# Tile 2's hidden layer from seven half-size products, its preparation moved into the searched list

## The chip, the cores and the metric

The kernel runs on one core of a Trainium2 chip. The metric is the time on the device in microseconds (us), median of several runs; the kernel before takes 837.97 us (three runs, 837.77 to 838.3). A profile is one more execution, taken by the hardware profiler.

## The reference

Attention in chunks of 64 tokens, then a two-layer network with h·cos(h) between the layers. In the core of it:

```python
scores = scale * np.matmul(q_c, k_c.transpose(0, 1, 2, 4, 3))   # chunks of 64 tokens, 8 heads of 64
attn = np.exp(scores - np.max(scores, axis=-1, keepdims=True))
attn = attn / (np.sum(attn, axis=-1, keepdims=True) + 1e-09)
x = np.matmul(attn, v_c)          # laid out as (4608 tokens, 512)
h = x @ w_in                      # (4608, 512) @ (512, 2048)
g = h * np.cos(h)
out = g @ w_out                   # (4608, 2048) @ (2048, 512)
```

All of it is float32.

## The kernel before, in words

The 4608 tokens are nine tiles of 512 (tile 0 to tile 8). The 2048 hidden features are 16 blocks of 128 (`fc`). To keep float32 accuracy at the fast matmul format, every operand is kept as a high and a low part, and every product is three matmuls: high·high, high·low, low·high.

**Ordinary tiles.** For one block, `hidden` (line 514) issues 12 matmuls of 512 columns into one PSUM bank of the pair named `h`; `activated` (525) makes g = h·cos(h) in six steps that alternate between ScalarE (ACT) and VectorE (DVE): whole turns, minus those turns, sine, times h (after which the bank is free), high part, low part. `projected_by_parts` (564) multiplies g with the block of w_out: four parts of three 512-column matmuls into the four banks `acc`. The projection of a step follows its hidden product three steps later (`LAG`).

**Pairs of blocks by seven products.** From tile `FAST` on, two blocks are taken together (`pair`, 776): h of the two is a two-by-two block product that is formed from seven products of half size (A11, S3, S2, A12, A22, S1, S4 in that order, six matmuls of 256 columns each) and a few additions. It needs seven combinations of x (`halves`, 707: four differences on DVE, seven high parts on ACT, seven low parts on DVE) and seven of w_in for each of eight pairs of blocks. The combinations of w_in are formed once, on GpSimd (POOL) with the high parts on ACT (`whole_again`, `sums_of_w`, `parts_of_sums`, 645 to 670), kept in HBM (`combo`), and streamed back for every tile, two products (512 KB) a load, through `load_two` (696) into rooms that the resident w_in leaves free. Room `fc` is free once the four sums of its pair have gone out (`keep_sums`, 681). SyncE (SP) issues every DMA in program order.

**What sets the order.** The kernel begins with a list of pieces (`piece`, 1001): weight preparation, attention of tiles 0 to 2, and hidden and projection of tile 0 (blocks 0 to 7), tile 1, and tile 0 again (blocks 8 to 15), which is 32 hidden steps and 29 projections. `in_order` (138) places the pieces by assumed lengths and due times, then tries 1,500 random changes of the due times and keeps what ends no later. After the list, tile 2 runs in a written loop (1249 to 1274) as an ordinary tile: beside its 16 steps the loop issues the attention of tile 3 (two bursts of small matmuls, `burst`, 964), the combinations of x for tile 3 and of w_in for the pairs 0 to 4. Tiles 3 to 8 run through `pair`; the pairs 5 to 7 of w_in are combined during the first of them. Before the first pair of a tile, `run_of_short` (913) issues the scores of the next tile, a run of 128 small matmuls into both `h` banks and both `a` banks; DVE's `m` (largest, 384) and `e` (scores minus largest, 388) read them out and free the banks, and the first product A11 needs one of the two `h` banks.

Of the kernel before, what the change touches and what calls it, by code (L numbers as in the profile page):

```python
# [21 lines left out]
P = 128  # L22
# [8 lines left out]

GROUP = 8


SCORES = 0
WEIGHTED = 12
LAST_TURN = 5

FAST = 3


STREAM = 5
# [1 line left out]

H_ROOM = 3
G_ROOM = 4
X_ROOMS = {1: (0, 1, 2), 0: (13, 14, 15)}

EARLY = 2

# [15 lines left out]
IDLE = 3.0  # L66

AHEAD = 4.0
TRIALS = 1500


def placed(work, after_it, rank):
# [65 lines left out]
def in_order(work, next_tile):  # L138

    after_it = [[] for _ in work]  # L140
    for i, w in enumerate(work):
        for a in w[3]:
            after_it[a].append(i)
    matmuls = [i for i, w in enumerate(work) if w[0] == PE and w[1] > LONG]

    due = [1e9] * len(work)
    clock = 0.0
    for i in matmuls:
        due[i] = clock
# [12 lines left out]
    chance = random.Random(1)  # L162
# [11 lines left out]
def attention_then_cos_ffn(ctx: ExitStack, tc, qT, kT, v, w_in, w_out, out, wide):  # L174
# [25 lines left out]
    def kept(ins):  # L200
        tc.keep_in_program_order(ins)
        return ins
# [337 lines left out]
            lambda: kept(nc.vector.tensor_tensor(g_lo, g, g_hi.bitcast(F32), op=ALU.subtract)),  # L540
        ]

    def activate(t, fc, h, most):
        whole, turn, sine, times, high, rest = activated(t, fc, h)
        whole()
        turn()
        take(soon, 1)
        sine()
        times()
        take(soon, 1)  # L550
        take(full, 2)
        high()
        rest()
        take(full, len(full))
        take(soon, most)
        take(late, len(late))

    def project(s):
        sums_out = []
        for run in projected_by_parts(s, sums_out):  # L560
# [28 lines left out]
    def finish(t, sub, o, whole):  # L589
        r0 = t * TOK + sub * P  # L590
        to = out[r0 : r0 + P, :]
        if not whole:

            os, to = att.tile([P, DM], F32, name="vt" if sub % 2 else "pts"), partial[sub]
        elif t == 0:
            os = acc["partial", sub]
        elif t < NT - 1 and t != FAST - 1:
            os = out_room(sub)
        else:

            if sub % 2 == 0:
                acc["x"] = x_room(t + 2 if t < FAST else t + 1, F32)
            os = acc["x"][:, sub % 2]
        if whole and t == 0:
            kept(nc.vector.tensor_tensor(os, os, o, op=ALU.add))
        elif t < FAST - 1 and sub % 2 == 0 or t == NT - 1 and sub % 2:
            kept(nc.scalar.copy(out=os, in_=o))
        else:
            kept(nc.vector.tensor_copy(os, o))
        nc.sync.dma_start(out=to, in_=os)  # L610

    def resume():

        for sub in range(NSUB):
            os = acc["partial", sub] = out_room(sub)
            nc.sync.dma_start(out=os, in_=partial[sub])

# [19 lines left out]

    sums_w = {}  # L640

    def pool(out, a, b, op):
        kept(nc.gpsimd.tensor_tensor(out, a, b, op=op))

    def whole_again(k):

        one, two = in_halves(k)
        for j, a in ((A11, one[:, :, 0]), (A12, one[:, :, 1]), (A22, two[:, :, 1])):
            store(combo(k, j), a)
        sums_w[k] = [dec.tile([P, 2, HALF], F32, name="w") for _ in range(2)]  # L650
        for w, a in zip(sums_w[k], (one, two)):
            pool(w, a[:, 0].bitcast(F32), a[:, 1].bitcast(F32), ALU.add)

    def sums_of_w(k):
        w1, w2 = sums_w[k]
        u, v = sums_w[k] = [wts.tile([P, 2, HALF], F32, name=f"half{i}") for i in range(2)]
        pool(u[:, 0], w2[:, 0], w2[:, 1], ALU.add)
        pool(u[:, 1], w1[:, 0], w2[:, 0], ALU.subtract)
        pool(v[:, 0], u[:, 0], w1[:, 0], ALU.subtract)
        pool(v[:, 1], w1[:, 1], v[:, 0], ALU.subtract)  # L660

    def parts_of_sums(k):

        one, two = in_halves(k)
        u, v = sums_w.pop(k)
        rooms = [(u[:, 0], two[:, :, 0]), (u[:, 1], one[:, :, 0]), (v[:, 0], one[:, :, 1]), (v[:, 1], two[:, :, 1])]
        for a, room in rooms:
            kept(nc.scalar.copy(out=room[:, 0], in_=a))
        for a, room in rooms:
            pool(room[:, 1], a, room[:, 0].bitcast(F32), ALU.subtract)  # L670

    def combine(k):

# [33 lines left out]
    def halves(t):  # L707
# [40 lines left out]
    def halves_in_turn(t):  # L748
        difference, high, low = halves(t)
        return [  # L750
            lambda: (difference(S1), high(A11)), lambda: (difference(S3), high(S1)),
            lambda: (difference(S2), high(S3)), lambda: (difference(A22), high(S2)),
            lambda: (low(A11), high(A12)), lambda: (low(S3), high(A22)), lambda: (low(S2), high(S4)),
            lambda: low(A12), lambda: low(A22), lambda: low(S1), lambda: low(S4),
        ]


    due_parts = deque()
# [202 lines left out]

    pieces = {}

    def attend(t, step):

        if step == 9:
            for hp in range(2, HP):
                load_v(t, hp)
        if step == 3:
            soon.extend(lambda hp=hp: total(t, hp) for hp in range(HP))  # L970
            soon.append(lambda: inverse(t))

        for hp in {4: (0, 1), 5: (2,), 6: (3,)}.get(step, ()):
            soon.append(lambda hp=hp: quotient(t, hp))
        if 4 <= step < 12:
            hp, odd = divmod(step - 4, 2)
            if not odd:
                pieces["turn"] = turned(t, hp)
            soon.extend(pieces["turn"][4 * odd : 4 * odd + 4])

    def burst(t, scored):


# [141 lines left out]
    ahead = early(1)  # L1125


    def attend_third(begin, room):

        t = 2  # L1130
        below = []
        for g in range(2):
# [16 lines left out]
        for g in range(2):  # L1149
# [14 lines left out]
            if g == 0:  # L1164
# [1 line left out]
                    for hp in (2, 3):  # L1166
                        load_v(t, hp)
                piece(SP, 0.1, values_next, w)
            for i in (0, 2):
                hi = piece(ACT, 0.45, rest_of(key, i), w, room)  # L1170
                banks_free["a", i // 2] = piece(DVE, 0.6, rest_of(key, i + 1), hi)
                x_done.setdefault(t, []).append(banks_free["a", i // 2])

        def queries_next():
            for hp in range(HP):
                load_qk(t + 1, hp)

        def values_after():
            for hp in range(2):
                load_v(t + 1, hp)  # L1180

        piece(SP, 0.1, values_after, piece(SP, 0.1, queries_next, w))


    stream = None
# [2 lines left out]
    projected = {}  # L1188
    partial_out = []
    out_of = {}  # L1190
    for s in range(STAGE):
        t, fc = order[s]
        key = ("h", s)
# [11 lines left out]
        if s >= LAG:  # L1205
# [9 lines left out]
            if order[u + 1][0] != tu:  # L1215
                for sub in range(NSUB):
                    done = piece((DVE if sub % 2 else ACT), 0.6, rest_of(key, sub), stream,
                                 *(split.values() if u > GROUP else [ahead[HP - 1]]))
                    out_of[u + 1, sub] = done
                    if u < GROUP:  # L1220
                        partial_out.append(done)
                if u < GROUP:
# [4 lines left out]
                else:  # L1227
                    piece(SP, 0.1, resume, *(out_of[u + 1, sub] for sub in range(NSUB)))
# [9 lines left out]
        given[s] = a  # L1238
        if s == GROUP + 7:
            begin = hid  # L1240
        if s == GROUP + NFC - 1:
            attend_third(begin, hid)

    for i in in_order(work, x_done[2]):
        work[i][2]()


    through = STAGE - 1 - LAG
    for s in range(STAGE, STAGE + NFC):
        t, fc = order[s]  # L1250
        h = hidden(t, fc)
        attend(t + 1, fc)
        if s - LAG > through:
            through += 1
            full.extend(project(through))
        if fc in (SCORES, WEIGHTED):
            burst(t + 1, fc == SCORES)
            through += 1
            full.extend(project(through))
        activate(t, fc, h, {WEIGHTED + 1: 2, WEIGHTED + 2: 0, WEIGHTED + 3: 1}.get(fc, 4))  # L1260
        if fc == WEIGHTED:
            soon.extend(halves_in_turn(t + 1))
            prefetch(t + 2)
            take(soon, 2)
        if fc == 2:
            exponentials(t + 1)
        take(full, len(full))

        if fc in (3, 5, 7, 9, 11):
            combine((fc - 3) // 2)  # L1270
        if fc == 13:
            parts_of_sums(4)
        if fc >= 7 and fc % 2:
            keep_sums((fc - 7) // 2)
# [82 lines left out]
```

## Time and profile before

| | |
|---|---|
| median of three runs | 837.97 us |
| profiled execution | 837.58 us |
| its span, first to last instruction | 835.8 us |
| mean granted TensorE clock | 0.998 |
| busy: PE / weight loads / DVE / ACT / POOL | 819.9 / 712.0 / 632.9 / 462.9 / 82.0 us |
| chain that ended last | PE 87%, ACT 5%, DVE 4%, DMA 2% |

The profiled execution lies 0.39 us under the median of the runs, and 1.78 us of it lie outside the span. Times in rows are us from the span's start. PE is the matmul engine, PEld its weight loads. In the chain of waits, "x12" counts matmuls that are merged into a row.

### The profile page before, as it was taken

The page shows a single profiled execution, that of the slowest core. Times are in us where ns is not written, and L with a number is a line of the kernel's source. Part 1 is how long each engine was busy: PE and PEld are TensorE (multiplying, and loading weights), DVE is VectorE, ACT ScalarE, POOL GpSimd, SP SyncE. Part 2 cuts the span into 40 slices and gives each one's busy share as a digit, 9 for nine tenths or more (in the row PEclk, how much of TensorE's full clock was granted, in tenths as well). Part 3 has the DMA queues.
Part 4 walks back from the last instruction along what each step waited for, and adds up shares of the span by engine and source line. Part 5 has one row for each costly group of instructions (what it writes and reads, how often), then busy time and mean ns, then how long its engine had stood idle before and what let it go on. Part 6 is the DMA issues. An engine that isn't in the chain of part 4 may idle for free.

```text
span 835.8 us, 16892 instructions
## 1 busy us (share of the span) xinstructions
PE 819.9 (98%) x6656; PEld 712.0 (85%) x6656; DVE 632.9 (76%) x1198; ACT 462.9 (55%) x928; POOL 82.0 (10%) x92
## 2 busy tenths in 40 slices
PE   5999999999999999999999999999999999999998
PEld 5777888888888878888998899889988899899996
DVE  6969888843698589977898788968896889665443
ACT  5999973333434636564645564465446454644443
POOL 1010000000069454400000000000000000000000
PEclk9999999999999999999999999999999999999999
DMA  9991200430245678986856675676657575456521
GB/s 338 415 414 43 77 1 1 134 118 1 79 161 202 213 228 313 325 316 209 277 175 227 202 257 177 206 240 210 215 179 249 189 250 177 152 176 227 177 76 50
DMA packets 65998, 160.47 MB, mean 192 GB/s; under 512 B 6528, under 2 KB 20864, under 8 KB 65920
## 3 DMA queue, kind: packets, MB, share of 16 engines
q1 hardware_dynamic: 65920, 159.41, 55.5%
q8 instruction: 52, 0.85, 0.4%
q14 instruction: 26, 0.21, 0.1%
HBM read 134.22 MB, written 25.17 MB: 191 GB/s over the span
## 4 chain that ended last, share of the span: by engine, by line
PE 87%; ACT 5%; DVE 4%; DMA 2%; issue 1%; SPq 0%; ACTq 0%; DVEq 0%
PE acc L208 44%; PE h L208 42%; DMA w_in<-in_w_in_dram 2%; PE a L208 1%; DMA qt<-in_qT_dram 1%; ACT half L278 1%; ACT w L276 1%; DVE g L536 1%; ACT g_hi L539 0%; ACT g L537 0%; DVE g L538 0%; SPq L205 0%; ACT g L535 0%; ACT w_out L286 0%; ACT L395 0%
## 5 line engine op out<-in xcount | busy, mean ns | idle before, releaser
L208 PE MATMUL acc<-w_out,g_hi 128*128 128x512 f32 x960 | 299.5, 393 | 0.0
L208 PE MATMUL h<-x,w_in 128*128 128x256 f32 (+1 forms) x1728 | 290.1, 317 | 2.0 <-DVE e L388 1.6
L208 PEld LDWEIGHTS h<-x,w_in 128*128 128x128 f32 x1728 | 255.3, 188 | 34.5 <-issue 2.3
L208 PEld LDWEIGHTS acc<-w_out,g_hi 128*128 128x128 f32 x960 | 171.8, 188 | 31.0
L208 PE MATMUL acc<-w_out,g_lo 128*128 128x512 f32 x480 | 187.4, 390 | 0.0
L827 ACT ACTIVATE g<-g 128x256 f32<-128x256 f32 x144 | 70.6, 490 | 113.8 <-DVE g L823 113.8
L208 PE MATMUL h<-w_in,w_in 128*128 128x256 f32 x864 | 118.5, 281 | 0.5 <-DVE w_in L814 0.4
L208 PEld LDWEIGHTS h<-w_in,w_in 128*128 128x128 f32 x864 | 110.8, 188 | 6.5 <-DVE w_in L814 3.0
L208 PEld LDWEIGHTS acc<-w_out,g_lo 128*128 128x128 f32 x480 | 90.1, 188 | 19.7
L811 ACT COPY h<-h 128x256 f32<-128x256 f32 x96 | 34.3, 357 | 117.4 <-PE h L208 115.9
L208 PE MATMUL acc<-w_out,w_in 128*128 128x512 f32 x288 | 73.7, 393 | 0.0
L842 DVE TENSOR_TENSOR g_lo<-g,g_hi 128x512 fp32r<-128x512 f32 x72 | 49.2, 686 | 22.7 <-ACT g_hi L838 21.6
L814 DVE TENSOR_TENSOR w_in<-h,w_in 128x256 f32<-128x256 f32 x96 | 36.2, 419 | 36.6 <-ACT x L740 18.7
L208 PEld LDWEIGHTS acc<-w_out,w_in 128*128 128x128 f32 x288 | 51.1, 188 | 8.8
L451 DVE STREAM_TRANSPOSE pts<-e 32x256 f32<-32x256 f32 x128 | 55.5, 435 | 1.9
L536 DVE SCALAR_TENSOR_TENSOR g<-g,h 128x512 f32<-128x512 int32 x48 | 32.8, 684 | 30.5 <-ACT g L535 29.9
L535 ACT ACTIVATE g<-h 128x512 int32<-128x512 f32 x48 | 28.6, 595 | 41.8 <-PE h L208 41.7
L830 DVE TENSOR_TENSOR g<-w_in,g 128x512 f32<-128x512 f32 x48 | 34.3, 714 | 17.4 <-ACT g L827 17.4
L539 ACT CAST g_hi<-g 128x512 fp32r<-128x512 f32 x48 | 29.9, 622 | 30.0 <-DVE g L538 25.1
L540 DVE TENSOR_TENSOR g_lo<-g,g_hi 128x512 fp32r<-128x512 f32 x48 | 35.5, 740 | 14.4 <-ACT g_hi L539 13.1
L830 DVE TENSOR_TENSOR g<-h,g 128x256 f32<-128x256 f32 x96 | 40.3, 420 | 8.0 <-ACT g L827 7.0
L823 DVE SCALAR_TENSOR_TENSOR g<-g,h 128x256 f32<-128x256 int32 x96 | 39.8, 415 | 8.6 <-ACT g L820 8.0
(108 smaller groups left out, 924.3 us busy)
## 6 DMA issues: line engine op xcount, KB each, us to landing
w_in<-combo SPq DMA_DIRECT2D x168, 512.0 KB, 3.9
combo<-w_in SPq DMA_DIRECT2D x56, 256.0 KB, 4.5
qt<-in_qT_dram SPq DMA_DIRECT2D x36, 256.0 KB, 5.1
kt<-in_kT_dram SPq DMA_DIRECT2D x36, 256.0 KB, 5.3
w_in<-in_w_in_dram SPq DMA_DIRECT2D x16, 512.0 KB, 9.6
w_out<-in_w_out_dram SPq DMA_DIRECT2D x16, 512.0 KB, 9.9
vt<-in_v_dram SPq DMA_DIRECT2D x22, 256.0 KB, 4.7
out_dram<-w SPq DMA_DIRECT2D x14, 256.0 KB, 2.1
```

The costliest lines, as they stand in the source:

```text
L208: kept(nc.tensor.matmul(*args, **kw))
L451: kept(nc.vector.transpose(out=dst[o : o + BL, :, qb], in_=src[i : i + BL, :, kb]))
L535: lambda: kept(nc.scalar.activation(n, h, AF.Identity, bias=0.25, scale=0.5 / math.pi)),
L536: lambda: kept(nc.vector.scalar_tensor_tensor(g, n, -2.0 * math.pi, h, op0=turns, op1=over)),
L539: lambda: kept(nc.scalar.copy(out=g_hi, in_=g)),
L540: lambda: kept(nc.vector.tensor_tensor(g_lo, g, g_hi.bitcast(F32), op=ALU.subtract)),
L811: kept(nc.scalar.copy(out=out, in_=in_))
L814: kept(nc.vector.tensor_tensor(out, in_, ds, op=ALU.add))
L823: kept(nc.vector.scalar_tensor_tensor(g, g.bitcast(I32), -2.0 * math.pi, h, op0=ALU.mult, op1=ALU.add))
L827: kept(nc.scalar.activation(g, g, AF.Sin, bias=0.5 * math.pi))
L830: kept(nc.vector.tensor_tensor(g, h, g, op=ALU.mult))
L842: kept(nc.vector.tensor_tensor(lo, g, hi.bitcast(F32), op=ALU.subtract))
```

## The change

`FAST` becomes 2, so tile 2 goes through `pair` as well and its written loop is gone. What the loop did is in the list now: the combinations of x for tile 2 (`of_x`), and those of w_in for the pairs 0 to 4, pairs 0 and 1 on DVE (`BY_DVE`), pairs 2 to 4 on POOL (`BY_POOL`), one pair after another. The attention of tile 2 was in the list already; its last step is a plain copy on ACT instead of a split into high and low parts. The outputs of tile 1 wait for it, because they pass through its buffers `vt` and `pts`; the half sums of tile 0 come back into x's room. The search makes 4,000 trials and each changes due times in one stretch of time only. The rooms of the x combinations swap with the parity of the tiles.

```diff
-FAST = 3
+BY_DVE = 2
+BY_POOL = 3
+FAST = 2
...
-X_ROOMS = {1: (0, 1, 2), 0: (13, 14, 15)}
+X_ROOMS = {0: (0, 1, 2), 1: (13, 14, 15)}
...
-TRIALS = 1500
+TRIALS = 4000
...
-        far, some = chance.choice((1, 3, 8, 15)), chance.choice((0.02, 0.1, 0.3))
-        other = [d + (chance.gauss(0, far) if chance.random() < some else 0.0) for d in due]
+        far, some, long = (chance.choice(c) for c in ((1, 3, 8, 15), (0.05, 0.2, 0.5), (10, 30, 100, 300)))
+        first = chance.uniform(-long / 2, starts[matmuls[-1]])
+        other = [
+            d + (chance.gauss(0, far) if first < b < first + long and chance.random() < some else 0.0)
+            for d, b in zip(due, starts)
+        ]
...
-            for i in (0, 2):
-                hi = piece(ACT, 0.45, rest_of(key, i), w, room)
-                banks_free["a", i // 2] = piece(DVE, 0.6, rest_of(key, i + 1), hi)
+            for i in range(2):
+                banks_free["a", i] = piece(ACT, 0.55, rest_of(key, i), w)
...
+    for k in range(BY_DVE + BY_POOL):
+        by, eng, ls = (DVE, nc.vector, (1.38, 1.7)) if k < BY_DVE else (POOL, nc.gpsimd, (2.8, 3.4))
+        used = hids[GROUP + 2 * k + 1 + (NFC - GROUP if 2 * k >= GROUP else 0)]
+        a = piece(by, ls[0], lambda k=k, eng=eng: whole_again(k, eng), used, lows[-1], *split.values(), port=True)
+        a = piece(by, ls[1], lambda k=k, eng=eng: sums_of_w(k, eng), a, lag=2.0, port=True)
+        a = piece(ACT, 1.5, lambda k=k: high_parts(k), a)
+        lows.append(piece(by, ls[1], lambda k=k, eng=eng: low_parts(k, eng), a, port=True))
+        kept_sums[k] = piece(SP, 0.1, lambda k=k: keep_sums(k), lows[-1], lag=3.0)
...
+    ready = x_done[2] + [hids[GROUP + NFC - 1], kept_sums[0], kept_sums[1]]
+    ready += [out_of[GROUP + NFC, sub] for sub in range(NSUB)]
+    for j in (S1, S3, S2, A22):
+        a = whole_x[j] = piece(DVE, 0.69, of_x(0, j), a, *ready, port=True)
+    for j in (A11, S3, S2, A12, A22, S1, S4):
+        a = piece(ACT, 0.55, of_x(1, j), whole_x.get(j, whole_x[S1]))
+        parts_x.append(piece(DVE, 0.69, of_x(2, j), a, port=True))
-    for i in in_order(work, x_done[2]):
+    for i in in_order(work, parts_x + [kept_sums[k] for k in range(3)]):
         work[i][2]()
...
-    through = STAGE - 1 - LAG
-    for s in range(STAGE, STAGE + NFC):
-        t, fc = order[s]
-        h = hidden(t, fc)
-        attend(t + 1, fc)
...
-        if fc in (3, 5, 7, 9, 11):
-            combine((fc - 3) // 2)
...
-    for u in range(through + 1, STAGE + NFC):
+    for u in range(STAGE - LAG, STAGE):
         due_parts.extend(projected_by_parts(u, full))
     for t in range(FAST, NT):
```

On TensorE the list keeps its order, but for the second weighted run of tile 2, which moves from ahead of hidden step 25 to ahead of step 26. At the list's end two things stand otherwise.

On DVE, before the change, these rows precede the read-out of the first scores run ahead of a tile of seven products (tile 3); L536, L538 and L540 are steps of g, L744 the low parts of tile 3's x combinations, L384 and L388 the read-out `m` and `e`:

```order
L540 TENSOR_TENSOR g_lo<-g,g_hi 128x512
L536 SCALAR_TENSOR_TENSOR g<-g,h 128x512
L744 TENSOR_TENSOR w_in_3037<-vt,w_in_3037 128x512
L538 TENSOR_TENSOR g<-h,g 128x512
L744 TENSOR_TENSOR w_in_3038<-pts,w_in_3038 128x512
L540 TENSOR_TENSOR g_lo<-g,g_hi 128x512
L744 TENSOR_TENSOR w_in_3039<-e_2331,w_in_3039 128x512
L384 TENSOR_REDUCE m<-h 128x8
L388 TENSOR_TENSOR e_2296<-h,m 128x8x64
```

With the change the same place, now at the end of the list ahead of tile 2 (L541, L543 and L545 are the steps of g, L743 the low part of an x combination, L389 and L393 the read-out):

```order
L743 TENSOR_TENSOR w_in_2141<-vt,w_in_2141 128x512
L543 TENSOR_TENSOR g<-h,g 128x512
L541 SCALAR_TENSOR_TENSOR g<-g,h 128x512
L543 TENSOR_TENSOR g<-h,g 128x512
L545 TENSOR_TENSOR g_lo<-g,g_hi 128x512
L541 SCALAR_TENSOR_TENSOR g<-g,h 128x512
L545 TENSOR_TENSOR g_lo<-g,g_hi 128x512
L543 TENSOR_TENSOR g<-h,g 128x512
L545 TENSOR_TENSOR g_lo<-g,g_hi 128x512
L389 TENSOR_REDUCE m<-h 128x8
L393 TENSOR_TENSOR e_2427<-h,m 128x8x64
```

The low parts of x stood between the last steps of g and directly ahead of the read-out; they stand before the last two steps of g now.

On ACT, before the change, the four high parts of w_in's pair 4 (L668) stand two steps of g ahead of the first copy of a tile of seven products (L811):

```order
L668 CAST w_in_1128<-half_2887 128x256
L668 CAST w_in_1082<-half_2887 128x256
L668 CAST w_in_1082<-half_2888 128x256
L668 CAST w_in_1128<-half_2888 128x256
L535 ACTIVATE g<-h 128x512
L740 CAST w_in_3039<-e_2331 128x512
L537 ACTIVATE g<-g 128x512
L539 CAST g_hi<-g 128x512
L535 ACTIVATE g<-h 128x512
L537 ACTIVATE g<-g 128x512
L539 CAST g_hi<-g 128x512
L811 COPY h<-h 128x256
```

With the change (L540, L542 and L544 are steps of g, L661 the high parts of pair 4, L801 that copy):

```order
L544 CAST g_hi<-g 128x512
L540 ACTIVATE g<-h 128x512
L542 ACTIVATE g<-g 128x512
L544 CAST g_hi<-g 128x512
L661 CAST w_in_1104<-half_2335 128x256
L661 CAST w_in_1079<-half_2335 128x256
L661 CAST w_in_1079<-half_2336 128x256
L661 CAST w_in_1104<-half_2336 128x256
L801 COPY h<-h 128x256
```

The high parts of pair 4 have moved behind the last step of g, directly ahead of the first copy.

## Rows read from the trace of the kernel before

**Rows 1.** Page, part 1: busy us, share of the span, instructions.
```profile
PE 819.9 (98%) x6656; PEld 712.0 (85%) x6656; DVE 632.9 (76%) x1198; ACT 462.9 (55%) x928; POOL 82.0 (10%) x92
```

**Rows 2.** Timeline of PE: start, length, work, count [idle before, releaser].
```profile
203.93 2.88 PE L208 MATMUL h<-x,w_in 128*128 128x512 f32 x12
...
290.04 2.88 PE L208 MATMUL h<-x,w_in 128*128 128x512 f32 x12
...
296.93 0.27 PE L208 MATMUL h<-kt,qt 64*64 64x64 f32 x1
...
299.01 0.72 PE L208 MATMUL acc<-w_out,g_hi 128*128 128x512 f32 x2
...
302.22 1.65 PE L208 MATMUL h<-x,w_in 128*128 128x256 f32 x12 [1.56 <-DVE e L388]
...
308.67 0.87 PE L208 MATMUL h<-w_in,w_in 128*128 128x256 f32 x6
...
386.99 0.27 PE L208 MATMUL h<-kt,qt 64*64 64x64 f32 x1
...
475.33 0.27 PE L208 MATMUL h<-kt,qt 64*64 64x64 f32 x1
```

**Rows 3.** Chain of waits in order of time: start, length, what.
```profile
233.54 2.72 PE h L208 x12
236.26 2.72 PE acc L208 x12
...
499.98 2.08 PE acc L208 x9
502.06 2.82 PE h L208 x24
...
510.44 2.08 PE acc L208 x9
```

**Rows 4.** Page, part 5: a group of weight loads, busy us, mean ns.
```profile
L208 PEld LDWEIGHTS h<-w_in,w_in 128*128 128x128 f32 x864 | 110.8, 188 | 6.5 <-DVE w_in L814 3.0
```

**Rows 5.** Timeline of DVE ahead of tile 3's first product.
```profile
294.00 1.55 DVE L540 TENSOR_TENSOR g_lo<-g,g_hi 128x512 fp32r<-128x512 f32 x1
...
299.52 1.23 DVE L744 TENSOR_TENSOR w_in<-e,w_in 128x512 fp32r<-128x512 f32 x1
...
301.38 0.69 DVE L388 TENSOR_TENSOR e<-h,m 128x512 f32<-128x512 f32 x1
```

**Rows 6.** Timeline of POOL: a cycle of w_in's combinations, and the last before tile 3.
```profile
262.80 3.08 POOL L643 TENSOR_TENSOR w_in<-half,w_in 128x256 fp32r<-128x256 f32 x4 [0.17 <-ACT w_in L668]
...
272.81 3.04 POOL L643 TENSOR_TENSOR w_in<-half,w_in 128x256 fp32r<-128x256 f32 x4 [1.07 <-ACT w_in L668]
...
289.59 3.67 POOL L643 TENSOR_TENSOR w_in<-half,w_in 128x256 fp32r<-128x256 f32 x4 [10.41 <-ACT w_in L668]
```

**Rows 7.** Timeline of SP, then DMA issues from 295 to 296.3: KB each, us to landing.
```profile
290.72 2.92 SPq L638 DMA_DIRECT2D combo<-w_in  x4
295.19 1.05 SPq L205 DMA_DIRECT2D w_in<-combo  x2
...
w_in<-combo SPq DMA_DIRECT2D x2, 512.0 KB, 4.4
```

**Rows 8.** Timelines of ACT and DVE: the step of g whose hidden product ended at 201.21.
```profile
204.27 0.62 ACT L539 CAST g_hi<-g 128x512 fp32r<-128x512 f32 x1 [0.82 <-DVE g L538]
...
204.92 0.69 DVE L540 TENSOR_TENSOR g_lo<-g,g_hi 128x512 fp32r<-128x512 f32 x1 [0.74 <-ACT g_hi L539]
```

**Rows 9.** Windows 130 to 165 and 165 to 200: busy us of each engine, summed.
```profile
sum 70.00, PE 70.00 PEld 57.66 DVE 45.74 ACT 25.73 POOL 0.00; mean PE 35.00 PEld 28.83 DVE 22.87 ACT 12.87 POOL 0.00
```

**Rows 10.** Groups of DVE, 230 to 300 (POOL at work): busy us, mean ns.
```profile
L540 DVE TENSOR_TENSOR g_lo<-g,g_hi 128x512 fp32r<-128x512 f32 x13 | 11.5, 883 | 3.3 <-ACT g_hi L539 2.8
...
L451 DVE STREAM_TRANSPOSE pts<-e 32x256 f32<-32x256 f32 x16 | 7.0, 435 | 0.2
```

**Rows 11.** Waits of PE: engine line, waited for: us in total, times, longest.
```profile
PE a L430 <- DVE x L501: 1.1, 2, 0.9
```

More of the change, by code (lines that the diff above doesn't have):

```diff
@@ L541, in activated @@
         ]
[L543 to L556, printed above, removed]
     def project(s):
@@ L591, in finish @@
         to = out[r0 : r0 + P, :]
-        if not whole:
-            os, to = att.tile([P, DM], F32, name="vt" if sub % 2 else "pts"), partial[sub]
+        if t == 1 or not whole:
+            os = att.tile([P, DM], F32, name="vt" if sub % 2 else "pts")
+            to = to if whole else partial[sub]
         elif t == 0:
             os = acc["partial", sub]
-        elif t < NT - 1 and t != FAST - 1:
+        elif t < NT - 1:
             os = out_room(sub)
@@ L605, in finish @@
             kept(nc.vector.tensor_tensor(os, os, o, op=ALU.add))
-        elif t < FAST - 1 and sub % 2 == 0 or t == NT - 1 and sub % 2:
+        elif t < FAST and sub % 2 == 0 or t == NT - 1 and sub % 2:
             kept(nc.scalar.copy(out=os, in_=o))
@@ L614, in resume @@
         for sub in range(NSUB):
-            os = acc["partial", sub] = out_room(sub)
-            nc.sync.dma_start(out=os, in_=partial[sub])
+            if sub % 2 == 0:
+                acc["x"] = x_room(0, F32)
+            os = acc["partial", sub] = acc["x"][:, sub % 2]
+            load(os, partial[sub])
     HALF = TOK // 2
@@ L640, in attention_then_cos_ffn, with whole_again @@
     sums_w = {}
-    def pool(out, a, b, op):
-        kept(nc.gpsimd.tensor_tensor(out, a, b, op=op))
-    def whole_again(k):
+    def whole_again(k, eng=nc.gpsimd):
         one, two = in_halves(k)
@@ L651, in whole_again, with sums_of_w, rooms_of_sums, high_parts @@
         for w, a in zip(sums_w[k], (one, two)):
-            pool(w, a[:, 0].bitcast(F32), a[:, 1].bitcast(F32), ALU.add)
-    def sums_of_w(k):
+            kept(eng.tensor_tensor(w, a[:, 0].bitcast(F32), a[:, 1].bitcast(F32), op=ALU.add))
+    def sums_of_w(k, eng=nc.gpsimd):
         w1, w2 = sums_w[k]
         u, v = sums_w[k] = [wts.tile([P, 2, HALF], F32, name=f"half{i}") for i in range(2)]
[L657 to L660, printed above, removed]
-    def parts_of_sums(k):
[L664 to L670, printed above, removed]
+        for out, a, b, op in (
+            (u[:, 0], w2[:, 0], w2[:, 1], ALU.add), (u[:, 1], w1[:, 0], w2[:, 0], ALU.subtract),
+            (v[:, 0], u[:, 0], w1[:, 0], ALU.subtract), (v[:, 1], w1[:, 1], v[:, 0], ALU.subtract),
+        ):
+            kept(eng.tensor_tensor(out, a, b, op=op))
+    def rooms_of_sums(k):
+        one, two = in_halves(k)
+        u, v = sums_w[k]
+        return [(u[:, 0], two[:, :, 0]), (u[:, 1], one[:, :, 0]), (v[:, 0], one[:, :, 1]), (v[:, 1], two[:, :, 1])]
+    def high_parts(k):
+        for a, room in rooms_of_sums(k):
+            kept(nc.scalar.copy(out=room[:, 0], in_=a))
+    def low_parts(k, eng=nc.gpsimd):
+        for a, room in rooms_of_sums(k):
+            kept(eng.tensor_tensor(room[:, 1], a, room[:, 0].bitcast(F32), op=ALU.subtract))
+    def parts_of_sums(k):
+        high_parts(k)
+        low_parts(k)
     def combine(k):
@@ L746, in halves @@
         return difference, high, low
[L748 to L755, printed above, removed]
     due_parts = deque()
@@ L962, in attention_then_cos_ffn @@
     pieces = {}
[L964 to L979, printed above, removed]
     def burst(t, scored):
@@ L1125, in attention_then_cos_ffn, with attend_third @@
     ahead = early(1)
-    def attend_third(begin, room):
+    def attend_third(begin):
         t = 2
@@ L1176, in queries_next @@
                 load_qk(t + 1, hp)
[L1178 to L1182, printed above, removed]
+        piece(SP, 0.1, queries_next, w)
+        return w
     stream = None
@@ L1190, in attention_then_cos_ffn @@
     out_of = {}
+    hids = []
+    third = None
     for s in range(STAGE):
@@ L1217, in attention_then_cos_ffn @@
                     done = piece((DVE if sub % 2 else ACT), 0.6, rest_of(key, sub), stream,
-                                 *(split.values() if u > GROUP else [ahead[HP - 1]]))
+                                 *(split.values() if u > GROUP else [ahead[HP - 1]]), third)
                     out_of[u + 1, sub] = done
@@ L1226, in attention_then_cos_ffn @@
                     piece(SP, 0.1, values_third, *partial_out)
-                else:
-                    piece(SP, 0.1, resume, *(out_of[u + 1, sub] for sub in range(NSUB)))
         key = ("g", s)
@@ L1238, in attention_then_cos_ffn @@
         given[s] = a
+        hids.append(hid)
         if s == GROUP + 7:
-            begin = hid
-        if s == GROUP + NFC - 1:
-            attend_third(begin, hid)
-    for i in in_order(work, x_done[2]):
-        work[i][2]()
-    through = STAGE - 1 - LAG
-    for s in range(STAGE, STAGE + NFC):
-        t, fc = order[s]
-        h = hidden(t, fc)
-        attend(t + 1, fc)
[L1253 to L1267, printed above, removed]
-        if fc in (3, 5, 7, 9, 11):
-            combine((fc - 3) // 2)
[L1271 to L1274, printed above, removed]
@@ L1277, in attention_then_cos_ffn @@
-    for u in range(through + 1, STAGE + NFC):
+            third = attend_third(hid)
+    piece(SP, 0.1, resume, hid)
+    kept_sums = {}
+    lows = [None]
+    for k in range(BY_DVE + BY_POOL):
[6 more added lines that the diff above has]
+        kept_sums[k] = piece(SP, 0.1, lambda k=k: keep_sums(k), lows[-1], lag=3.0)
@@ new lines, in of_x, with run @@
+    def of_x(i, *args):
+        def run():
+            if "x" not in made:
+                made["x"] = halves(2)
+            made["x"][i](*args)
+        return run
+    ready = x_done[2] + [hids[GROUP + NFC - 1], kept_sums[0], kept_sums[1]]
+    ready += [out_of[GROUP + NFC, sub] for sub in range(NSUB)]
+    whole_x = {}
+    a = None
+    for j in (S1, S3, S2, A22):
+        a = whole_x[j] = piece(DVE, 0.69, of_x(0, j), a, *ready, port=True)
+    parts_x = []
+    for j in (A11, S3, S2, A12, A22, S1, S4):
+        a = piece(ACT, 0.55, of_x(1, j), whole_x.get(j, whole_x[S1]))
+        parts_x.append(piece(DVE, 0.69, of_x(2, j), a, port=True))
```

8 lines of the change are left out of this document (3 added, 5 removed).

## The prediction

> **What bounds the kernel.** I read the page's busy shares first, then the timeline of PE at the seams between tiles, then the chain of waits in order of time, and last the timelines of the engines that feed PE at the seam that waits. PE is busy 819.9 of 835.8 us [rows 1], at a mean granted clock of 0.998 of full speed, and the chain is 87% PE by the page's part 4. In the chain matmuls follow each other without a hole: an ordinary step is 2.72 us of hidden product and 2.72 us of projection, and a pair by seven products comes round every 510.44 - 499.98 = 10.46 us [rows 3]. So the kernel is bound by the matmuls it issues, and an edit on another engine counts only where it makes PE wait. After the first 80 us one wait of PE is over 1 us: A11, the first product of tile 3, waits 1.56 us for DVE's `e` [rows 2]. Differences of 0.2% (1.7 us) are about what a measurement of this kernel tells from none.
>
> **Tile 2's matmuls.** A 512-column matmul takes 2.72 / 12 = 0.2267 us, a 256-column one 2.82 / 24 = 0.1175 us [rows 3]. Two blocks cost 24 x 0.2267 = 5.44 us the old way and 42 x 0.1175 = 4.94 us by seven products: 0.5 us a pair, 4.0 us for eight. That is the upper end. The nearest rows for the whole stage give less. Call S the moment at which all hidden products of a tile are issued and three projections of it are left. In the list S is 203.93, where tile 2's first hidden product begins; one tile later it is 290.04 + 2.72 + 2.72 = 295.48, after the last hidden product and one more projection [rows 2]. Tile 2 thus takes 91.55 us. Tile 3 takes 386.99 - 295.48 = 91.5 us, and tile 4 takes 475.33 - 386.99 = 88.34 us [rows 2]. Tile 3 is dearer than tile 4 because it carries the pairs 5 to 7 of w_in and the 1.56 us. With the change tile 2 becomes that dear first tile and tile 3 an ordinary one of 88.34 us, so one 91.55 is exchanged for one 88.34: a gain of 3.2 us. I take this, since it is the whole stage with its seams, and keep 4.0 as the upper end.
>
> The Trainium skill, TensorE: Matmul & The Clock Gate, section Back-to-back issue gap, speaks against the change: in streams of weight load and matmul it gives about 81 ns a matmul at 128 columns and 131 ns at 512. Interpolated (an estimate from that page) that is 98 ns at 256 columns, so a pair would cost 42 x 98 = 4.1 us against 24 x 131 = 3.1 us, and the change would lose 7.8 us on the tile. The rows disagree with it, 226.7 ns and 117.5 ns here, and they decide.
>
> **The wait of A11.** Before tile 3, DVE did the last low parts of x and of g while POOL formed combinations. A low part of g took 1.55 us and the last low part of x 1.23 us, and `e` ended at 301.38 + 0.69 = 302.07, just before A11 at 302.22 [rows 2, 5]. The order shows that with the change the low parts of x stand before the last two steps of g, and only the low part of the last step precedes `m` and `e`. That part ended 204.92 + 0.69 - 201.21 = 4.4 us after its hidden product in the list [rows 8]; the last hidden product of the list ends at S - 2.72, so DVE is free at S + 1.7. The scores run begins at S + 1.45 (296.93 - 295.48) and takes 2.08 us, to 299.01 [rows 2], so its first half is there at S + 2.5; `m` and `e` of it, two instructions of 0.69 us [rows 5], end at S + 3.9, or S + 4.4 with half a microsecond for the hand-overs. PE reaches A11 at 302.22 - 1.56 - 295.48 = S + 5.2. So I book the whole 1.6 us as gained; 0.8 us of slack covers it, and the other end is that all 1.6 stays. What is late next is checked below.
>
> **The last pair of w_in before tile 2.** The seventh product S4 of tile 2's first pair reads combinations that are loaded into room 8, which the sums of pair 4 must have left. Before, POOL finished pair 4 at 289.59 + 3.67 = 293.26, SP issued the load at 295.19 (1.93 later), it landed 4.4 us after, at 299.6, and S4 ran at 308.67 [rows 2, 6, 7]: 9 us to spare. With the change ACT does the high parts of pair 4 only behind the last step of g. A g_hi ends 204.27 + 0.62 - 201.21 = 3.7 us after its hidden product [rows 8], here at S + 1.0; after the first cast, half to all of a g_hi's 0.62 us, POOL can start, and takes 3.08 to 3.67 us [rows 6], to S + 4.4 or S + 5.3. With 1.93 and 4.4 us on top room 8 is full at S + 10.7 to 11.6. S4 comes 308.67 - 302.22 = 6.45 us behind A11, at S + 11.6. The 9 us have shrunk to between 0 and 0.9, and I book nothing; the bounds are 0 and 2.7 us (a slip of ACT by one 2.72 us piece of PE). The four casts themselves stand ahead of ACT's first copy of tile 2, which is wanted only after A11 and S3, at S + 6.6, so they hold nothing up unless POOL's sums of pair 4 are late. Those come from a chain of pairs 2, 3, 4 that starts when DVE has done pair 1, some 42 us before S by the order, and a pair takes 272.81 - 262.80 = 10 us [rows 6]: about 30 us of POOL and some waits for ACT, hence 5 to 10 us early.
>
> **What the list takes on.** DVE gets pairs 0 and 1 (each two instructions of 512 elements at 0.69 and eight of 256 at between half and all of that, 4.1 to 6.9 us a pair), four differences and seven low parts (11 x 0.69 = 7.6 us), and loses four splits (2.8 us): 13 to 19 us net. From 130 to 200 it is busy 45.7 of 70 us [rows 9], so it comes to 59 to 65 of 70. A step of 5.44 us asks 2.1 us of DVE for g, and the bank that its `times` frees is wanted a whole step later, so delays of 2 to 3 us are covered. The second weighted run stands one step later on PE, which makes room for its transposes. ACT gains 20 casts of half length, each under 0.62 us [rows 8], in a stretch where it is busy 25.7 of 70. The longest wait that PE has in the list after its first hidden product, 1.1 us in two parts [rows 11], may fall or grow with another search; I book 0 between a gain of 2 us (that wait and as much again in smaller ones) and a loss of 3 us (half a step, DVE late for one weighted run). The 28 more loads of 512 KB, 14.7 MB, fall into tile 2's pairs; tile 4 streams as much and keeps its 88.34 us.
>
> **The sum.** The profiled execution has 835.8 of span and 1.78 outside. 835.8 - 3.2 - 1.6 = 831.0, with 1.78 it is 832.8, and the median lies 0.39 above that execution: 833.2 us.
>
> **Rivals.** (1) A11 still waits, because DVE comes late out of the fuller list: 834.8. For it speaks that the wait stood at the same seam, against it that POOL's last low parts begin after S + 1.3, beside PSUM reads. (2) The list or S4 gives back about 3 us: 836.2, near no change. The thin margin of S4 speaks for it, the whole step of cover for g against. (3) The wider search also removes the early waits: 831.3. (4) Slower: DVE falls behind in the last eight steps of the list. There it has 24 instructions of g, two copies and 11 of x, 37 x 0.69 = 25.5 us, and 8 transposes of 0.435, together 29 us in 43.5 us, beside 27 to 30 us of POOL. A low part of g took 1.55 instead of 0.69 us when it met POOL [rows 5]. If every microsecond of POOL stopped DVE, DVE would need 56 to 59 us and PE would wait 12.5 to 15 us, for 833.2 + 13.7 = 847. It decides once collisions cost DVE more than 14.5 us, and turns the sign once they cost some 19. Against it: from 230 to 300 the low parts averaged 0.883 us [rows 10], 13 x 0.19 = 2.5 us in all.
>
> By the Trainium skill, SBUF — State Buffer, section Who interferes with whom, a DVE instruction with two SBUF inputs and a POOL instruction that reads SBUF exclude each other, and the second waits for the whole first. The 1.55 us agrees with it; the mean in rows 10 says that few instructions meet so, and that rival keeps a small chance.
>
> (5) Matmuls of 256 columns are held to their weight loads in tile 2: at 188 ns a load [rows 4] a pair costs 42 x 0.188 = 7.9 us, 2.5 more than now, and the tile 19.7 more: 833.2 + 3.2 + 19.7 = 856. The 117.5 ns of the later tiles say that loads overlap.
>
> **Chances.** Forecast 0.56 (own range 832.0 to 834.4), rival 1 0.15, rival 2 0.12, rival 3 0.12, rival 4 0.04, rival 5 0.01. The range runs from 831.0 to 836.2. Faster by over 0.2% means under 836.3: the forecast, rivals 1 and 3, and a little of 2, 0.86; within 0.2% 0.09; slower 0.05.
>
> **What would show it.** Right: the list's last projection ends within 1 us of 204, matmuls of 256 columns follow it at 117.5 ns, no wait on `e` ahead of tile 2's A11, bursts of scores 88.3 us apart from tile 3 on. Wrong: a row of PE waiting for DVE `g` or `pts` between 130 and 204; a gap ahead of S4 in the first pair with a load of room 8 landing late; `e` of tile 3's scores ending later than 5 us after S; low parts of g at 1 us and more through the last 40 us of the list.

## The result, and the profile after

The changed kernel takes 840.8 us (median of six runs, 839.84 to 841.4) against 837.77 us for the kernel before (six runs, 836.77 to 838.3): a ratio of 1.0036 with a 95% interval of 1.0023 to 1.0049. It is slower by 0.36%; 833.2 us was forecast. The profiled execution has a span of 838.1 us (839.84 us in all), 2.3 us more than before.

The page's part 1 (busy us, share of the span, instructions), beside [rows 1]:

```profile
PE 817.9 (98%) x6800; PEld 715.4 (85%) x6800; DVE 654.2 (78%) x1259; ACT 474.4 (57%) x973; POOL 63.4 (8%) x72
```

PE is busy 2.0 us less and the span is 2.3 us longer, so PE waits 4.3 us more. The timeline of PE, with the seams that stand in [rows 2] (start, length, work, count, and in brackets the idle time before it and what ended it):

```profile
189.09 3.02 PE L213 MATMUL h<-x,w_in 128*128 128x512 f32 x12 [0.81 <-DVE g L543]
...
196.66 3.02 PE L213 MATMUL h<-x,w_in 128*128 128x512 f32 x12 [1.82 <-DVE g L543]
...
203.49 0.74 PE L213 MATMUL h<-x,w_in 128*128 128x512 f32 x2 [1.08 <-DVE g L543]
...
210.54 0.27 PE L213 MATMUL h<-kt,qt 64*64 64x64 f32 x1
...
214.06 1.11 PE L213 MATMUL h<-x,w_in 128*128 128x256 f32 x8
...
220.43 0.76 PE L213 MATMUL h<-w_in,w_in 128*128 128x256 f32 x5
...
233.49 0.74 PE L213 MATMUL h<-x,w_in 128*128 128x256 f32 x4 [1.04 <-DVE g L820]
...
299.86 0.27 PE L213 MATMUL h<-kt,qt 64*64 64x64 f32 x1
...
388.21 0.27 PE L213 MATMUL h<-kt,qt 64*64 64x64 f32 x1
```

Read it against the prediction's S. The scores run of tile 3 stands at 210.54, so S at the end of the list is 210.54 - 1.45 = 209.1; it was 203.93. Tile 2 then takes 299.86 - 209.1 = 90.8 us (before 91.55, forecast 89.9) and tile 3 takes 388.21 - 299.86 = 88.35 (before 91.5, forecast 88.34). A11 at 214.06 and S4 at 220.43 have no wait. The list gave away 5.2 us, tiles 2 and 3 brought 3.9 of the 4.8 us, and what follows 388.21 is 1.1 us longer; the sum is the 2.3 us of the span.

Most of the 5.2 us arise late in the list. The first burst of tile 2's scores, on PE before and after:

```profile
108.97 1.16 PE L208 MATMUL a<-kt,qt 64*64 64x64 f32 x64
```

```profile
109.48 1.16 PE L213 MATMUL a<-kt,qt 64*64 64x64 f32 x64
```

There the list is 0.5 us late. From there to S it takes 99.61 us (209.09 - 109.48) where it took 94.96 (203.93 - 108.97), 4.65 us more. The three brackets ahead of 210 are 3.7 of these; the rest goes at the same places, for the product that begins behind such a wait takes 3.02 to 3.05 us, against 2.88 in [rows 2], and about 0.3 us a wait are lost beside the idle time. As [rows 11], the waits of PE (total, times, longest):

```profile
PE h L213 <- DVE g L543: 3.7, 3, 1.8
...
PE acc L213 <- ACT pts L598: 0.6, 1, 0.6
```

L543 is `times`, which frees the bank of h. Why DVE came late stands in the chain of waits that leads to the third of them (start, length, what):

```profile
177.40 2.73 PE h L213 x12
...
180.22 0.19 ACT g L540
180.41 4.65 DMA out_dram<-pts
...
185.15 0.60 DVE pts L733
...
199.39 1.15 DVE w_in L743
200.54 1.14 DVE g_lo L545
201.68 1.15 DVE w_in L743
202.83 0.61 DVE g L543
...
203.49 3.06 PE h L213 x12
```

A store of finished output stands in the middle of the path to a matmul. Once it has landed, DVE has work up to the third wait's end at 203.49, with three pauses for ACT of 1.7 us together. The rows of DVE, then of ACT, then of SP's queue around it:

```profile
177.39 1.28 DVE L600 COPY vt<-acc 128x512 f32<-128x512 f32 x2
185.15 0.69 DVE L733 TENSOR_TENSOR pts<-e 128x512 f32<-128x512 f32 x1 [6.48 <-DMA out_dram<-pts]
```

```profile
185.88 0.63 ACT L739 CAST w_in<-pts 128x512 fp32r<-128x512 f32 x1 [5.06 <-DVE pts L733]
```

```profile
173.07 2.85 SPq L631 DMA_DIRECT2D combo<-w_in  x4
178.44 0.33 SPq L210 DMA_DIRECT2D w_in<-combo  x1
178.82 1.54 SPq L631 DMA_DIRECT2D combo<-w_in  x3
180.41 1.07 SPq L601 DMA_DIRECT2D out_dram<-pts  x1
```

The S1 difference of tile 2's x is written to a `pts` buffer, and the change made `finish` stage tile 1's output there (the condition `t == 1 or not whole`). DVE stands 6.48 us until the store has landed; ACT stands 5.06 us behind DVE, and its sine and the casts of w_in stand behind that. The store is late because SP issues in order: ahead of it stand a load that waits until pair 2's four stores have landed, and three more stores.

A second store does the same on a smaller scale in tile 2's second pair. The chain that leads to the wait at 233.49:

```profile
217.09 4.19 DMA w_in<-combo
221.30 9.47 DMA combo<-w_in
230.84 0.41 ACT w_in L661
231.27 1.28 ACT L817
...
233.01 0.44 DVE g L820
233.49 1.71 PE h L213 x12
```

ACT may cast pair 5's sums into w_in's room only after the unchanged blocks of that pair have left it. SP issues the three stores of these blocks from 219.84 on, behind five loads of 512 KB, and they take long to land (DMA issues from 216 to 224; over the whole kernel the median is 4.5):

```profile
combo<-w_in SPq DMA_DIRECT2D x3, 256.0 KB, 9.6
```

So the casts are late, and the sine behind them too.

### The profile page after: what moved, and what is told of

Its sections match the earlier page's. It is cut to its first block, busy times and chain, and to the rows that moved or that the text cites. A ratio compares the mean times of both kernels' runs of the same rounds, so it can differ in the third digit from the quotient of the medians.

```text
span 838.1 us, 17300 instructions
## 1 busy us (share of the span) xinstructions
PE 817.9 (98%) x6800; PEld 715.4 (85%) x6800; DVE 654.2 (78%) x1259; ACT 474.4 (57%) x973; POOL 63.4 (8%) x72
## 4 chain that ended last, share of the span: by engine, by line
PE 83%; DMA 9%; ACT 4%; DVE 2%; issue 1%; SPq 1%; POOL 0%; ACTq 0%; DVEq 0%
PE acc L213 42%; PE h L213 40%; DMA w_out<-in_w_out_dram 4%; DMA kt<-in_kT_dram 2%; DMA combo<-w_in 1%; PE a L213 1%; DMA out_dram<-pts 1%; DMA vt<-in_v_dram 1%; ACT half L283 1%; DMA w_in<-combo 1%; ACT g_hi L544 0%; DVE w_in L743 0%; ACT w L281 0%; SPq L210 0%; DVE x L743 0%
## 5 line engine op out<-in xcount | busy, mean ns | idle before, releaser
L213 PE MATMUL h<-x,w_in 128*128 128x256 f32 (+1 forms) x1728 | 270.3, 305 | 4.8 <-DVE g L543 3.7
L817 ACT ACTIVATE g<-g 128x256 f32<-128x256 f32 x168 | 82.3, 490 | 131.8 <-DVE g L813 131.8
L213 PE MATMUL h<-w_in,w_in 128*128 128x256 f32 x1008 | 138.2, 281 | 0.0
L213 PEld LDWEIGHTS h<-w_in,w_in 128*128 128x128 f32 x1008 | 129.4, 188 | 6.8 <-DVE w_in L804 2.7
L801 ACT COPY h<-h 128x256 f32<-128x256 f32 x112 | 40.0, 357 | 136.7 <-PE h L213 135.3
L213 PE MATMUL acc<-w_out,w_in 128*128 128x512 f32 x336 | 85.9, 393 | 0.0
L832 DVE TENSOR_TENSOR g_lo<-g,g_hi 128x512 fp32r<-128x512 f32 x84 | 57.5, 686 | 23.6 <-ACT g_hi L828 22.2
L810 ACT ACTIVATE g<-h 128x256 int32<-128x256 f32 x112 | 42.8, 382 | 8.2 <-PE h L213 4.3
L828 ACT CAST g_hi<-g 128x512 fp32r<-128x512 f32 x72 | 45.0, 624 | 0.0
L456 DVE STREAM_TRANSPOSE e<-e 32x256 f32<-32x256 f32 x96 | 41.8, 435 | 1.8
L813 DVE SCALAR_TENSOR_TENSOR g<-g,w_in 128x512 f32<-128x512 int32 x56 | 38.6, 689 | 0.0
```

Source lines behind the costliest of these rows:

```text
L213: kept(nc.tensor.matmul(*args, **kw))
L456: kept(nc.vector.transpose(out=dst[o : o + BL, :, qb], in_=src[i : i + BL, :, kb]))
L801: kept(nc.scalar.copy(out=out, in_=in_))
L810: kept(nc.scalar.activation(g.bitcast(I32), h, AF.Identity, bias=0.25, scale=0.5 / math.pi))
L813: kept(nc.vector.scalar_tensor_tensor(g, g.bitcast(I32), -2.0 * math.pi, h, op0=ALU.mult, op1=ALU.add))
L817: kept(nc.scalar.activation(g, g, AF.Sin, bias=0.5 * math.pi))
```

## The experiments

Unless said otherwise each is the changed kernel with one edit. Its times stand against the kernel before on the same chip (837.61 us for the first four runs, 837.55 for the last four); the changed kernel itself was not run there, and differences from its 840.8 us go across chips.

**Other rooms for S1 and S3.** The order of the instructions stays.

```diff
-            kept_x[j] = temporary("pts" if j in (S1, S2) else "vt")
+            if t == 2 and j in (S1, S3):
+                if "own" not in kept_x:
+                    kept_x["own"] = w_in_room(H_ROOM, F32)[:, PAD : PAD + 2 * TOK]
+                kept_x[j] = ...   # one half of that room each
```

> The changed kernel, with the first two differences of tile 2's x (S1 and S3) written into the room of w_in 3, which is idle then, instead of the pts and vt buffers that still hold tile 1's outputs; the order on all engines stays that of the changed kernel. Theory A (DVE stands 6.5 us behind the store of tile 1's output, because the store is issued late): the 6.48-us wait ahead of the S1 difference goes, the three waits of PE on g's times (0.81 + 1.82 + 1.08 = 3.7 us) shrink to under 1 us together, the scores run begins 3 to 4 us earlier (210.5 to about 207), and the kernel takes 837 us (836.3 to 838). Rival B (DVE has too much to do in the last 40 us of the list, with two pairs of w_in more and low parts at 1.1 to 1.2 us beside POOL): the wait moves but PE still waits 3 us or more on g, 840 to 841 us.

Measured 836.05 us, ratio 0.9979 (0.9970 to 0.9988): 4.8 us off the changed kernel's 840.8, and a little better than the 836.3 to 838 expected. The timeline of DVE shows no wait ahead of the difference:

```profile
178.53 1.28 DVE L600 COPY vt<-acc 128x512 f32<-128x512 f32 x2
179.73 1.12 DVE L739 TENSOR_TENSOR w_in<-e 128x512 f32<-128x512 f32 x1
```

None of the three waits on g is left in the list, and nothing was taken off DVE's work. The first burst of tile 2's scores and the scores run of tile 3:

```profile
110.61 1.16 PE L213 MATMUL a<-kt,qt 64*64 64x64 f32 x64
...
207.03 0.27 PE L213 MATMUL h<-kt,qt 64*64 64x64 f32 x1
```

The scores run stands at 207.0, as expected. From the burst to S (207.03 - 1.45 = 205.58) it takes 94.97 us, as before the change (94.96): all 4.65 us are gone. Theory A holds: without the wait DVE's load alone (rival B) costs PE nothing. In tile 2 PE now waits 0.7 us on `times` and 1.2 us on a load of w_in.

**Tile 1's outputs on ACT's queue.**

```diff
-        nc.sync.dma_start(out=to, in_=os)
+        (nc.scalar if t == 1 else nc.sync).dma_start(out=to, in_=os)
```

> The changed kernel, with tile 1's four outputs stored through ACT's DMA queue right behind the copies instead of through SP's, where they stand behind the stores of pair 2's combinations. Nothing else moves. Theory A: the stores are issued at about 178.5 to 179.5 instead of 180.4 and land 2.5 to 4 us later, so DVE's wait ahead of the S1 difference falls from 6.5 to between 2.5 and 4.5 us, PE's three waits on g from 3.7 to between 0.5 and 2.5 us, and the time is 838 to 839.5 us. Rival B (load and contention of DVE): no change, 840 to 841 us. Should ACT's own waits for DVE's copies hold up its sines, it may come out at 841 or more; then ACT's row ahead of the sine shows it.

Measured 835.5 us, ratio 0.9971 (0.9961 to 0.9981). Here the buffer is still shared, and only the queue and the moment of the stores change. ACT's queue, then DVE:

```profile
177.63 0.38 ACTq L601 DMA_DIRECT2D out_dram<-pts  x1
```

```profile
177.65 1.28 DVE L600 COPY vt<-acc 128x512 f32<-128x512 f32 x2
180.18 0.69 DVE L733 TENSOR_TENSOR pts<-e 128x512 f32<-128x512 f32 x1 [1.25 <-DMA out_dram<-pts]
```

The store leaves 2.8 us earlier (3.0 against DVE's copies, which begin 0.26 us later here) and is through within 2.55 us (180.18 - 177.63) where it took 4.74 (185.15 - 180.41). Together that takes DVE's wait from 6.48 to 1.25 us; I expected 2.5 to 4.5, and 838 to 839.5 us. PE waits for g no more in the list. S is 206.32 - 1.45 = 204.87, and the stretch from the burst of scores (109.73) to it takes 95.14 us. Why the transfer itself is shorter, no run separates: here it has less traffic issued just ahead of it. The Trainium skill, DMA: Bandwidth & Descriptors, section Issuing engines are not separate DMA queues, says that issuing from several engines saves only time on the sequencer, "which is usually small relative to the DMA itself". Here, with SP's waits and the DMAs ahead of the store counted in, that time was 2.8 us, not small beside the 2.55 us of the DMA. The second late store is still there, on ACT and then on PE:

```profile
225.99 0.41 ACT L661 CAST w_in<-half 128x256 fp32r<-128x256 f32 x1 [1.21 <-DMA combo<-w_in]
```

```profile
229.99 0.39 PE L213 MATMUL h<-x,w_in 128*128 128x256 f32 x1 [1.53 <-DVE g L820]
```

**The new search in the kernel before**, and nothing else (4000 trials by stretches, seed 2).

> The kernel before, with the new search alone (4000 trials, each in a stretch of time, other seed) and nothing else of the change. Theory A: the search as such neither costs nor gives much; tile 2 begins at 203.9 +- 1 us and the time is 837.8 +- 1.2 us. Rival C (the new search finds orders that look good to the planner and are worse on the chip): tile 2 begins 2 to 5 us later, 840 to 843 us. Rival D (the new search is worth having by itself): 835 to 836.5 us.

Measured 838.08 us, ratio 1.0005 (0.9996 to 1.0014): no difference, as theory A has it. The scores run stands at 209.51, before at 209.46. In the kernel before, the search as such neither cost nor gave anything; with the longer list of the changed kernel that is another question, and the next run is about it.

**The old search in the changed kernel** (1500 trials over the whole list, seed 1).

> The changed kernel with the old search (1500 trials over the whole list, old seed). In the order that it finds, SP has tile 1's four output stores ahead of the stores of pair 2's combinations, and the S1 difference stands 4 instructions behind the second copy. Theory A: the store is then issued right behind its copy, DVE's wait ahead of S1 is under 3 us, PE waits on g under 1.5 us in the last 40 us of the list, and the time is 836.5 to 838.5 us if nothing else in this order is worse. Rival B (load and contention): PE still waits about 3.7 us on g, 840 to 841 us. If the old search is plainly poorer with the longer list, waits elsewhere in the list, between 100 and 180 us, show it.

Measured 852.18 us, ratio 1.0171 (1.0158 to 1.0185). The time is 14 us above what I expected, and late stores are in it twice. The outputs did stand ahead of pair 2's stores, but behind eight loads of tile 3's queries and keys, which I had not counted. SP, DVE, and ACT at the first pair of tile 2:

```profile
176.67 1.43 SPq L205 DMA_DIRECT2D qt<-in_qT_dram  x1
...
181.00 0.43 SPq L205 DMA_DIRECT2D kt<-in_kT_dram  x1
181.53 1.10 SPq L596 DMA_DIRECT2D out_dram<-pts  x2
```

```profile
187.34 0.69 DVE L728 TENSOR_TENSOR pts<-e 128x512 f32<-128x512 f32 x1 [6.42 <-DMA out_dram<-pts]
```

```profile
224.04 0.40 ACT L656 CAST w_in<-half 128x256 fp32r<-128x256 f32 x1 [6.36 <-DMA combo<-w_in]
```

The last row is the second kind of late store, this time for pair 4; PE waits 7.0 us behind it. From 220 to 230 the granted clock is 0.68, between TensorE's two levels of 1.2 and 2.4 GHz: after those 7.0 idle us the 24 matmuls of 256 columns from 226.12 on last 5.0 us, where the changed kernel has 3.0 (216.19 to 219.20). The list ends 6.3 us later than before (S 210.24), and tile 2 takes 101.8 us from S to S. So the order that the search finds decides what these stores cost, and nothing in the plan says how long the store of an output holds its buffer.

**Unchanged blocks stored one pair earlier, with the outputs on ACT's queue.**

```diff
+    def originals(k):
+        ...   # the three stores that whole_again(k) began with
     def whole_again(k, eng=nc.gpsimd):
-        one, two = in_halves(k)
-        for j, a in ((A11, one[:, :, 0]), (A12, one[:, :, 1]), (A22, two[:, :, 1])):
-            store(combo(k, j), a)
+        for i in (0, 1) if k == 0 else (k + 1,) if k < 5 else (k,) if k > 5 else ():
+            originals(i)
+        one, two = in_halves(k)
```

> The kernel with tile 1's outputs on ACT's queue, and beside that SP issues the stores of a pair's unchanged blocks of w_in (three of each pair 1 to 5) one pair earlier, so that those of pair 5 go out at about 190 us instead of 216, ahead of the loads that wait for PE to leave their rooms. Theory A2 (in tile 2's second pair ACT's casts of pair 5's sums wait 1.74 us for these three stores to land, the sine and DVE's times behind them come late, PE waits 1.5 us at 230): the casts run without a wait, PE's wait at 230 goes, tile 2 takes 89.9 instead of 91.4 us, and the time is 834.0 us (833.5 to 834.6). Rival E (that wait is ACT's table load and exponentials, or POOL's low parts, and the store only happens to land then): the wait of PE stays over 1 us, 835.5 us.

Measured 834.65 us, ratio 0.9965 (0.9953 to 0.9978). The wait at 230 is gone, and tile 2 takes 295.2 - 205.53 = 89.7 us from S to S, 1.7 less than with the queue alone (91.4). Rival E is out. The time lies at the upper edge of the 833.5 to 834.6 us expected. The medians differ by 0.85 us, and the intervals of their ratios overlap, so what this edit adds is shown by the trace and not by the time.

**All three edits together.**

> All three edits together: S1 and S3 in the room of w_in 3, tile 1's outputs on ACT's queue, the unchanged blocks stored one pair earlier. Theory A: room and queue cure the same wait of DVE, so together they give no more than either, and the time is that of the queue with the early stores, 834.0 us (833.3 to 834.6). Rival B (part of the list's loss is DVE's load, and the room takes off what the queue leaves): 832 to 833.

Measured 834.72 us, ratio 0.9969 (0.9957 to 0.9980): room and queue cure the same wait, as theory A has it, at 0.1 us above the range expected. The casts of pair 5 run in one piece, and the seams of PE stand at:

```profile
224.23 1.33 ACT L665 CAST w_in<-half 128x256 fp32r<-128x256 f32 x4
```

```profile
206.32 0.27 PE L213 MATMUL h<-kt,qt 64*64 64x64 f32 x1
...
294.54 0.27 PE L213 MATMUL h<-kt,qt 64*64 64x64 f32 x1
...
382.85 0.27 PE L213 MATMUL h<-kt,qt 64*64 64x64 f32 x1
```

From 130 to 200 its engines are busy, as [rows 9]:

```profile
sum 70.00, PE 70.00 PEld 57.66 DVE 60.13 ACT 33.07 POOL 26.39; mean PE 35.00 PEld 28.83 DVE 30.06 ACT 16.53 POOL 13.20
```

PE has no pause in these 70 us, with DVE at 60.13 and POOL at 26.39. In the same list the low parts of g average 0.85 us (176 to 206) instead of 0.69, while POOL works. DVE's load and its meetings with POOL are real, and here they are covered.

**Early blocks in the order of the old search.**

> The changed kernel with the old search, and the unchanged blocks stored one pair earlier; tile 1's outputs go as in the changed kernel. In the order of the old search ACT's casts of pair 4 waited 6.36 us for these stores and PE 7.02 us for ACT at 226. Theory A2: that wait of PE goes and the time falls from 852.2 to 845 us (843.5 to 846.5). Rival F (the wait is POOL late with pair 4's sums): 850 us or more.

Measured 849.76 us, ratio 1.0139 (1.0124 to 1.0155); 845 was expected, and of the 7 us hoped for 2.4 came. The casts wait for no store any more and PE's 7.0 us are gone, but in their place PE waits for loads of w_in:

```profile
PE h L208 <- DMA w_in<-combo: 5.8, 3, 3.2
```

```profile
232.00 1.62 PE L208 MATMUL h<-w_in,w_in 128*128 128x256 f32 x6 [3.22 <-DMA w_in<-combo]
```

In that order the sums of pair 4 are last, and the casts now wait for POOL (3.77 us, then 0.3 to 0.4 each). SP issues the next loads at 218.62, and the first pair of tile 2 waits for its weights three times, 2.29 and 0.29 us and then the 3.22 us ahead of S4. By the chain of waits POOL's low parts of pair 4 end at 223.28, their stores land at 228.44, and the load that S4 needs is issued behind that. So rival F is half right: POOL is late with pair 4's sums, but it holds PE through the loads and no longer through ACT. That is the wait ahead of S4 which the prediction feared, in another order than the one it was about. The profile is of the slowest of the four executions (852.63 us), and from 222 to 240 its granted clock is 0.72; in the median execution less may be lost there.

**Early blocks alone.**

> The changed kernel with nothing but the unchanged blocks stored one pair earlier. Theory A2: PE's wait of 1.04 us at 233 goes; SP's stores of tile 1's outputs stand behind three stores fewer or more of w_in but still behind the waiting stores of pair 2, so the three waits on g at 189 to 203 stay: 839.5 us (838.8 to 840.3). If the early stores also shift the outputs' issue, the wait ahead of S1 shows it.

Measured 839.32 us, ratio 1.0023 (1.0014 to 1.0032). The wait at 233 is gone; the early stores put the outputs' store back to 182.05, and it costs more:

```profile
186.84 0.69 DVE L737 TENSOR_TENSOR pts<-e 128x512 f32<-128x512 f32 x1 [7.75 <-DMA out_dram<-pts]
```

```profile
PE h L213 <- DVE g L543: 5.0, 3, 2.1
```

With that there are four settings of one suspect in the same order: DVE waits 0, 1.25, 6.48 and 7.75 us for the store, and PE waits 0, 0, 3.7 and 5.0 us for g. The stretch from the first burst of tile 2's scores to S takes 94.97, 95.14, 99.61 and 100.89 us (for the last, 212.24 - 1.45 - 109.90). Some 2.75 us are covered when PE's idle time is counted (6.48 - 3.7, 7.75 - 5.0); between the last two settings 1.27 us more of DVE's wait make the stretch 1.28 us longer, so each microsecond is paid in full there.

## Why the prediction was wrong

- **Tile 2's matmuls and A11's wait: right.** Tile 3 takes 88.35 us (88.34 forecast), A11 does not wait in any kernel with the new order (`e` ends at 213.17, 4.1 us behind S; 3.9 to 4.4 forecast), and tile 2 takes 89.7 us with the second late store gone (89.9 forecast). Matmuls of 256 columns kept the rate of [rows 3], so rival 5 did not occur.
- **S4 and room 8: right.** At 220.43 there is no wait. The margin was as thin as forecast (0 to 0.9 us): with the early blocks alone S4 waits 0.15 us.
- **What the list takes on: this step failed.** I booked 0 between -2 and +3; it was 5.2 us, beyond the bound, and a row of PE that waits for DVE's g, which I had named as a sign of being wrong, came three times. DVE's busy time was sized well, 59 to 65 of 70 us forecast and 60.13 with the waits out of the way. What I left out is that the change moved two buffers under a DMA: tile 1's outputs went from the buffers `w` and `half` to `pts` and `vt`, where the next writer is DVE's first difference. I counted busy microseconds of each engine and set the cover of 2 to 3 us against delays of the work, but I did not ask what each moved instruction waits for besides its inputs. A store that SP issued behind a waiting load and three other stores cost DVE 6.48 us. Two edits that leave DVE's work as it is show it as the cause: of the 4.65 us that the stretch to S lost, the other rooms take back all and ACT's queue all but 0.2. The other 0.5 us come earlier in the list.
- **Tile 2's pairs: 0.8 us short.** The same oversight with pair 5's unchanged blocks; I had followed SP's queue only for room 8.
- **Rival 4 (DVE falls behind through POOL) has the right place and sign and the wrong cause.** By the Trainium skill, SBUF — State Buffer, section Who interferes with whom, a DVE instruction with two SBUF inputs contends with a GpSimd instruction that reads SBUF. The rows agree, with 1.14 and 1.15 us a low part in the chain above, while POOL works (190.72 to 202.28). Such meetings cost PE nothing once the store is out of the way. In the changed kernel eight instructions between 191.10 and 202.83 take 1.11 to 1.23 us instead of 0.69, behind the store's wait and on the way to PE; no run takes them away and leaves the store late, so what part of the 4.65 us they add to is open. (The rival's upper end of PE's wait is 15.5 us by its own terms, not 15.)
- **Rivals 2 and 3.** Rival 2 named the list as one of two places and 3 us as the loss; the place was right, and the loss was larger. Rival 3 (the wider search removes the early waits) did not occur: at the first burst of tile 2's scores the changed kernel is 0.5 us late, and the search alone gave 838.08 us.
- **What is left.** With all three edits 834.72 us stand against 833.2. The list is still 0.9 us later than before (204.87 to 203.93), all of it ahead of the first burst of tile 2's scores (109.91 to 108.97): 0.6 of it is a wait of PE for ACT's copy of the first partial sums (L598, at about 88 us) in every kernel with the new order. From the issue of the last stores to the end of the span it takes 5.65 us in the changed kernel (832.45 to 838.1) and 5.48 with all edits (827.02 to 832.5), against 4.86 before (830.94 to 835.8). No run tells why; this stays open. The medians lie 0.96 us above the profiled execution for the changed kernel and 0.39 for the one before (0.19 with all six runs of it).

## What to carry to other kernels

When a change gives a buffer to another writer, look for the DMA that still reads it, and follow the queue on which that DMA is issued: its own length, the waits ahead of it, and then what stands in order behind the engine that waits. An engine's busy time can be sized rightly and the stage still be lost to one instruction at its head. A planner that knows instructions but not the landing of transfers can put a writer right behind a copy. A queue without waits for the store, or another room for the writer, cured that here; giving the planner the store as a step of its own was not tried.

## What was not expected of the hardware

A store of 256 KB through ACT's queue was through within 2.55 us of its issue; the same store through SP's took 4.74 us, with a load and three stores issued in the 2 us ahead of it. No run tells whether the queue or that traffic makes the difference. Three casts that waited 1.74 us for stores (1.21, 0.24 and 0.29) cost PE 1.53 us, with ACT's table load of 1.28 us and the sine in order behind them; when the casts ran without a wait, PE's wait was gone.
